# Pair 2's second product in three one-pass parts, passes ordered by form, and a new order of the steps

## The chip, the cores and the metric

The kernel runs on one core of a Trainium2 chip. The core has five engines that run side by side, each through its own list of instructions in order: TensorE (PE; its weight loads are shown apart as PEld), VectorE (DVE), ScalarE (ACT), GpSimd (POOL) and SyncE (SP, which here only starts DMA transfers). The metric is device time in microseconds, the median of several runs; lower is better.

## The reference

A gated linear recurrence is followed by a feed-forward layer. q, k, v, a_re and a_im have 4 batches, 8 heads, 768 positions and 48 channels in fp32. The weights w_in (384 x 2048) and w_out (2048 x 384) come in float64.

```python
mag = sqrt(a_re**2 + a_im**2);  scale = minimum(mag, 0.999) / (mag + 1e-6)
for t in range(S):                       # complex decay of a 48 x 48 state per batch and head
    S_re, S_im = ar*S_re - ai*S_im + k[t] v[t]^T,  ar*S_im + ai*S_re
    y[t] = q[t] @ S_re
x = y as (3072 tokens, 384)
h = x @ w_in
out = (h / (1 + exp(-h))) @ w_out        # (3072, 384)
```

## The kernel before

**Tiling.** The positions are cut into chunks of 128. There are 24 chunks (4 batches x 6), taken as 12 pairs (p = 0 to 11): chunks 2p and 2p + 1 have the same position in two batches. A chunk n first goes through the recurrence in its chunked form: gates for a pair at a time (steps G0 to Ga: magnitude, log decay, angle), running sums of log decay and angle by TensorE (`L`, `phase`), the floor of the sum (`floor`), its exponentials (`exp`), sine and cosine (`turn`, `trig`), the decayed and rotated k and q (`dk`, `dq`, `K`, `Q`), their transposes (`t`, `T` on TensorE for the first four chunks, then `tk`, `tq` on VectorE and `td` by DMA), the weights product and its mask (`w`, `m`), the output (`y`, put into xT by `x` and `xd`) and the state handed on to the same batch's next chunk (`s`, `ss`, `sd`, `S`).

**Feed-forward.** For a pair (256 tokens) the hidden layer is cut into eight blocks jp of 2 x 128 units. `h:p.jp` is the first product (6 fp32 matmuls of 128x256), `g:p.jp` the silu on ScalarE, `r:p.jp` the second product, which adds to accumulators of 128 tokens (m = 0, 1) by 384 columns. When all eight are added, the accumulators are evacuated and stored.

**Weights.** They are fetched as pairs of 32-bit words (`F`, SP's queue), and made fp32 by ScalarE (`R`, low word) and VectorE (`H`, high word; `J`, joined). 28 blocks are converted so in the first 120 us, in the order in which h and r need them.

**Two forms of the second product.** Pairs below PARTS (line 110) use fp32 matmuls (line 820), then `finish` (line 840) copies and stores. Later pairs split both operands. A head a keeps the high bits of g, the tail is b = g - a, and the difference form is gd = a - 4096 b; for the weights there are coarse = head, fine = 4096 x tail and diff = head - 4096 x tail. With u = a coarse + b fine and v = gd diff, the product is (1 + 1/4096) u - v / 4096, exactly the four terms of head and tail. All six operands are in the one-pass type fp32r, so a block takes three one-pass matmuls per weight tile instead of one fp32 matmul (lines 831, 835, 837). The steps for a block are `ga` (head of g, DVE), `gr` (its cast, ACT), `gb` (tail, DVE), `gc` (difference, DVE), `lw` (the weights' diff, loaded from DRAM over SP's queue) and `r`. The three forms of g have one buffer each (PBUF = 1, line 115) except in the last pair, the loaded diff has two. `ov` (line 846, ScalarE) scales one accumulator into SBUF, `oj` (line 850, VectorE) joins the other to it and stores.

**The weights' parts** are made once per block jp by `wh`, `wd`, `ws` (DVE: head, rest, diff), `wq`, `we` (ACT: coarse, fine) and `wk` (diff to DRAM, SP). fine takes over w2's buffers in a ring of nine, so it waits for the fp32 products that still read them. coarse, diff and the g forms lie in `room("right")` (line 879), in memory that the conversion's buffers give back.

**What sets the order.** The steps stand in one long string of 1861 names (lines 957 to 1098). Going through it, the program gives each step's instructions to their engines' lists; an engine never overtakes in its own list, and a DMA queue is served in order too. Waits come from data and from buffers that are still read. SP's queue holds fetches, loads, stores and the transposes of T alike, so an entry that waits holds those behind it.

Of the kernel before, what the change touches and what calls it, by code (L numbers as in the profile page):

```python
# [11 lines left out]
F32 = mybir.dt.float32  # L12
# [58 lines left out]
def kernel(  # L71
# [32 lines left out]
    Q = 32  # L104
# [5 lines left out]
    PARTS = 3  # L110
# [370 lines left out]
    def sums(n):  # L481

        x = X[n]
        first = n < STRAIGHT
        ps = (p_o if first else p_m).tile([C, DM], F32, tag="o" if first else "m", name=f"L{n}")
        running(ps, n, "l", upto if n < 2 else half, half_r)
        x["ek"] = att.tile([C, DM], F32, tag="L", name=f"L{n}")
        x["L"] = ps

    def floor(n):  # L490
        x = X[n]
        nc.vector.tensor_scalar(out=x["ek"], in0=x["L"], scalar1=L_MIN, scalar2=None, op0=ALU.max)
        x["L"] = x["ek"]

    def decays(n):

        x = X[n]
        x["eq"] = att.tile([C, DM], F32, tag="eq", name=f"eq{n}")
        x["decay"] = x["eq"]
        special(x["eq"], x["L"], AF.Exp)  # L500
        special(x["ek"], x["L"], AF.Exp, scale=-1.0)
# [322 lines left out]
    def result_of_parts(p, jp):  # L824
        x = A[p]
        a, b, d, t = (x[name, jp] for name in ("head", "tail", "gd", "diff"))
        last_ = jp == NJ // 2 - 1
        for m in range(2):
            u, v_ = (x["o"][2 * m + i].rearrange("p n c -> p (n c)") for i in range(2))
            for ji in range(2):  # L830
                nc.tensor.matmul(v_, lhsT=d[:, ji, ts(m, C)], rhs=t[:, ji],  # L831
                                 start=(jp == 0 and ji == 0), stop=(last_ and ji == 1))
            for ji in range(2):
                j = jp * 2 + ji
                nc.tensor.matmul(u, lhsT=a[:, ji, ts(m, C)], rhs=W["coarse"][:, j],  # L835
                                 start=(jp == 0 and ji == 0), stop=False)
                nc.tensor.matmul(u, lhsT=b[:, ji, ts(m, C)], rhs=W["fine", jp][:, ji],  # L837
                                 start=False, stop=(last_ and ji == 1))
# [7 lines left out]
    def o_scaled(p, m):  # L846
        ot = A[p]["ot", m] = moe.tile([C, 2, DM // 2], F32, tag="ot", name=f"ot{p}_{m}")
        nc.scalar.mul(ot, A[p]["o"][2 * m + 1], -FINER)

    def o_joined(p, m):  # L850
        ot, u = A[p]["ot", m], A[p]["o"][2 * m]
        halves = (slice(0, 1), slice(1, 2)) if p == NP - 1 else (slice(0, 2),)
        for i, n in enumerate(halves):
            nc.vector.scalar_tensor_tensor(out=ot[:, n], in0=u[:, n], scalar=1 + FINER,  # L854
# [24 lines left out]
    def room(side):  # L879
        if side not in later:  # L880
            (setup if side == "left" else conversion).close()
# [73 lines left out]
    with tc.manual_schedule():  # L955
        for x in """
                warm:30 re:0 re:1g im:0 e0:0 e1:0 e2:0 e3:0 re:2g hold: im:1 e0:1 e1:1 e4:0 e6:0
                e5:0 L:0 e2:1 e3:1 e4:1 e5:1 e6:1 e7:0 e8:0 q:0g k:0g exp:0 dq:0 warm:20 im:2g
                re:3g F: dk:0 e7:1 e8:1 at:0.0 an:0.0 phase:0 at:0.1 an:0.1 R: im:3g G0:1 turn:0
                trig:0 phase:1 turn:1 trig:1 L:1 exp:1 G5:1 G1:1 rk:0.0 warm:34 rq:0.0 t:0.2 t:0.0  # L960
                rq:0.1 t:0.3 T:0.3 T:0.2 G8:1 rk:0.1 q:1g k:1g dk:1 t:0.1 T:0.1 H: v:0g thirds:0
                rk:1.1 G7:1 rk:1.0 dq:1 ends:0 s:0 S:0 T:0.0 rq:1.1 rq:1.0 G2:1 G3:1 w:0.1 m:0.1
                F: H: R: w:0.0 m:0.0 t:1.1 t:1.3 T:1.3 T:1.1 t:1.2 T:1.2 t:1.0 T:1.0 v:1g G6:1
                G9:1 ends:1 last:0 thirds:1 q:2g v:2g k:2g k:3g s:1 y:0 x:0 w:1.1 w:1.0 G4:1 L:2
                L:3 exp:3 F: F: H: S:1 m:1.1 m:1.0 y:1 x:1 Ga:1 phase:2 phase:3 R: J: J: J: h:0.0
                h:0.1 F: sm:1 F: F: turn:2 last:2 exp:2 trig:2 R: H: dk:2 dq:2 rq:2.0 t:2.2 turn:3
                R: trig:3 rk:2.0 t:2.0 T:2.0 T:2.2 rk:2.1 t:2.1 s:2 dk:3 rq:2.1 t:2.3 rk:3.1 t:3.1
                w:2.0 g:0.1 R: T:2.3 rk:3.0 t:3.0 T:2.1 q:3g dq:3 rq:3.1 t:3.3 ends:2 S:2 rq:3.0
                t:3.2 g:0.0 T:3.1 T:3.0 J: H: J: H: T:3.3 m:2.0 w:2.1 m:2.1 r:0.0 H: w:3.1 T:3.2
                R: m:3.1 thirds:2 y:2 x:2 w:3.0 v:3g s:3 thirds:3 m:3.0 y:3 J: J: r:0.1 ends:3 F:  # L970
                F: F: H: R: R: R: x:3 h:1.0 sm:0 S:3 J: H: J: H: J: h:1.2 F: F: R: R: F: g:1.0 H:
                H: J: J: lk:0 lk:1 h:0.3 g:0.3 r:1.0 R: H: J: F: F: g:1.2 h:1.1 g:1.1 R: R: F: R:
                h:0.2 g:0.2 r:1.1 H: H: J: h:1.3 r:0.2 r:0.3 re:4g re:5g im:4g im:5g G0:2 G5:2
                G1:2 G2:2 H: wh:2 J: J: F: F: R: H: H: J: h:1.4 r:1.2 R: J: g:1.3 h:0.4 r:1.3 F:
                R: F: H: H: G7:2 G3:2 G4:2 L:4 R: J: J: F: F: H: R: J: g:1.4 r:1.4 H: G8:2 G6:2
                G9:2 Ga:2 F: F: F: carry:4 R: J: h:1.5 last:1 last:3 carried:4 phase:4 R: R:
                floor:4 H: H: J: exp:4 H: R: g:0.4 L:5 floor:5 k:4g im:6g q:4g h:0.5 r:0.4 exp:5
                turn:4 trig:4 g:1.5 F: R: g:0.5 J: h:1.7 h:0.7 g:0.7 g:1.7 carry:5 carried:5 dk:4
                phase:5 sm:2 F: R: last:4 ends:4 dq:4 J: K:4 tk:4 Q:4 tq:4 H: H: J: ends:5 F: R:
                turn:5 trig:5 k:5g lk:2 r:0.5 h:0.6 r:1.5 h:1.6 g:0.6 r:0.6 J: H: wd:2 we:2 J:  # L980
                dk:5 K:5 q:5g dq:5 Q:5 ws:2 td:4 g:1.6 r:1.6 wq:2 tk:5 tq:5 re:6g re:7g im:7g G0:3
                G8:3 G5:3 G1:3 G2:3 G7:3 G3:3 w:4.0 m:4.0 wh:1 r:0.7 of:0 w:4.1 m:4.1 v:4g s:4 S:4
                G6:3 y:4 x:4 td:5 carry:6 w:5.0 m:5.0 G9:3 w:5.1 m:5.1 v:5g y:5 x:5 q:6g G4:3 L:6
                floor:6 wh:0 wd:0 wh:4 Ga:3 carried:6 exp:6 r:1.7 of:1 wq:0 s:5 S:5 ws:0 xd:2
                h:2.1 wk:2 last:5 q:7g v:8 v:6g k:6g re:8g k:7g g:2.1 wq:1 h:2.0 wq:4 g:2.0
                phase:6 h:2.5 h:2.4 L:7 r:2.0 r:2.1 wd:1 ws:1 wk:1 turn:6 sm:3 ends:6 wk:0 last:6
                trig:6 we:0 g:2.5 dk:6 wh:3 K:6 s:6 g:2.4 wq:3 lk:3 dq:6 floor:7 exp:7 carry:7 k:8
                Q:6 carried:7 tk:6 tq:6 wd:4 ws:4 we:1 phase:7 h:2.2 g:2.2 wd:3 ss:6 ws:3 turn:7
                dk:7 trig:7 K:7 h:2.3 g:2.3 r:2.2 r:2.3 r:2.4 r:2.5 im:8g im:9g re:9g G0:4 G8:4
                G5:4 td:6 w:6.0 ends:7 dq:7 Q:7 tk:7 tq:7 we:4 h:2.7 G1:4 wk:4 we:3 wh:6 G7:4 wd:6  # L990
                ws:6 G2:4 G4:4 we:6 G3:4 wh:5 wd:5 m:6.0 G6:4 G9:4 wq:5 q:8 w:6.1 wq:6 m:6.1 y:6
                x:6 wk:3 sd:6 carry:8 Ga:4 q:9 last:7 v:7g s:7 ss:7 td:7 k:9 sd:7 sm:4 h:2.6 g:2.6
                S:6 ul:8 ws:5 w:7.0 m:7.0 w:7.1 m:7.1 g:2.7 we:5 y:7 x:7 wk:6 L:8 carried:8 ut:8
                floor:8 exp:8 S:7 r:2.6 phase:8 turn:8 trig:8 ul:9 lk:4 dk:8 K:8 tk:8 r:2.7 of:2
                xd:3 im:10 h:3.0 L:9 g:3.0 ends:8 dq:8 floor:9 exp:9 wh:7 wq:7 Q:8 tq:8 ga:3.0
                gb:3.0 h:3.1 h:3.2 gr:3.0 gc:3.0 lw:3.0 r:3.0 wk:5 carry:9 carried:9 ut:9 phase:9
                im:11 re:10 re:11 last:8 wd:7 ends:9 dq:9 g:3.1 ga:3.1 g:3.2 lw:3.1 turn:9 td:8
                h:3.4 h:3.3 ws:7 wk:7 k:11 gr:3.1 gb:3.1 gc:3.1 r:3.1 we:7 ga:3.2 dk:9 trig:9 Q:9
                K:9 G0:5 G5:5 w:8.1 w:8.0 gb:3.2 gc:3.2 tk:9 tq:9 g:3.3 g:3.4 ga:3.4 gr:3.2 G1:5
                G7:5 G2:5 h:3.5 lw:3.2 r:3.2 m:8.0 m:8.1 y:8 ga:3.3 gb:3.3 gc:3.3 G3:5 G6:5 G4:5  # L1000
                v:9 s:9 lw:3.3 gr:3.3 r:3.3 carry:10 last:9 td:9 G8:5 G9:5 Ga:5 k:10 carried:10
                ut:10 g:3.5 gb:3.4 gc:3.4 ss:9 x:8 h:3.7 g:3.7 phase:10 turn:10 h:3.6 g:3.6 ga:3.5
                sm:5 lk:5 w:9.0 m:9.0 w:9.1 trig:10 m:9.1 y:9 x:9 gr:3.4 carry:11 carried:11 ul:10
                s:8 ss:8 L:10 ga:3.6 floor:10 exp:10 lw:3.4 r:3.4 re:12 q:10 re:13 ut:11 phase:11
                gb:3.5 im:12 im:13 G0:6 lw:3.5 last:10 xd:4 h:4.1 gr:3.5 gc:3.5 r:3.5 G5:6 G1:6
                G2:6 gr:3.6 g:4.1 h:4.0 g:4.0 ends:10 dq:10 Q:10 dk:10 K:10 gb:3.6 G8:6 lw:3.6
                gc:3.6 r:3.6 tk:10 turn:11 ga:3.7 gr:3.7 tq:10 trig:11 gb:3.7 ul:11 G7:6 G3:6
                h:4.2 L:11 floor:11 exp:11 q:11 sd:8 g:4.2 h:4.3 g:4.3 G4:6 gc:3.7 lw:3.7 r:3.7
# [265 lines left out]
```

## Time and profile before

| | |
|---|---|
| time, median of 3 runs | 638.94 us (638.41 to 641.1) |
| the profiled execution | 642.44 us, of which the span from first to last instruction is 640.7 |
| granted TensorE clock, mean | 0.995 |
| fp32 second product, L820 | 192 records, 487 ns each (a fp32 matmul leaves two) |
| second product in parts, L831, L835, L837 | 288 recorded each (280 and 8 in other buffers), about 338 ns |
| first product, L716 | 1152 records, 381 ns |
| g forms on VectorE | head 426 ns, tail 684, difference 689 |
| g head's cast on ScalarE | 615 ns |
| weights' parts, per block | DVE 624 + 948 + 949 ns, ACT 825 + 834 ns |
| table loads on ScalarE | 77 of 1283 ns |
| DMA | 104.75 MB, mean 163 GB/s |

Busy times are shares of the span. The lengths of matmuls overlap, so the cost of a block is read from the start of one to the start of what follows. L numbers are lines of the kernel.

### The profile page before, as it was taken

What the parts mean: (1) busy time and instruction counts of PE and PEld (TensorE: products, weight loads), DVE (VectorE), ACT (ScalarE), POOL (GpSimd) and SP (SyncE); (2) the same over time, 40 slices, a digit from 0 to 9 for tenths busy, and PEclk for the clock granted to TensorE, in tenths of its full rate; (3) what the DMA queues carried; (4) which work ended last, traced back from release to release, by engine and by line L of the source; (5) the groups of instructions that cost most, each with busy time, mean ns of one, the idle gap of its engine ahead of it and who ended that gap; (6) DMA issues with size and microseconds to landing.
All of it is one profiled execution on the core that took longest, in us unless ns stands there. A gap on an engine that the chain in (4) does not pass through costs nothing.

```text
span 640.7 us, 11617 instructions
## 1 busy us (share of the span) xinstructions
PE 620.5 (97%) x3892; PEld 542.2 (85%) x3892; DVE 513.7 (80%) x875; ACT 417.1 (65%) x629; POOL 214.7 (34%) x368
## 2 busy tenths in 40 slices
PE   6899999999999999999999989999999998999996
PEld 4788876778777999899999979998988998999996
DVE  5998578858788998998999988988987885855744
ACT  7995398486696878939759848659579354323322
POOL 7341201633553325344224453243434422120000
PEclk8999999999999999999999999999999998999999
DMA  9766976756775896795797786897898573797782
GB/s 163 168 162 151 198 181 177 120 104 175 160 127 145 170 184 146 167 184 123 183 182 171 142 166 141 195 185 134 156 202 150 113 158 85 165 212 224 244 249 77
DMA packets 195111, 104.75 MB, mean 163 GB/s; under 512 B 167520, under 2 KB 173240, under 8 KB 195048
## 3 DMA queue, kind: packets, MB, share of 16 engines
q1 hardware_dynamic: 179944, 82.25, 55.7%
q0 software_dynamic: 11648, 17.20, 16.8%
q10 hardware_dynamic: 3456, 4.52, 2.1%
q8 instruction: 32, 0.52, 0.4%
q14 instruction: 31, 0.25, 0.2%
HBM read 77.21 MB, written 7.93 MB: 133 GB/s over the span
## 4 chain that ended last, share of the span: by engine, by line


## 5 line engine op out<-in xcount | busy, mean ns | idle before, releaser
L716 PE MATMUL h<-xT,w 128*128 128x256 f32 x1152 | 264.7, 381 | 1.0 <-DMA xT<-y 0.4
L716 PEld LDWEIGHTS h<-xT,w 128*128 128x128 f32 x1152 | 216.6, 191 | 32.8 <-ACT g L297 2.3
L562 POOL DMA_DIRECT2D T<-sq x120 | 78.2, 659 | 85.5 <-issue 39.4
L297 ACT ACTIVATE g<-h 128x512 f32<-128x512 f32 x96 | 55.8, 595 | 72.5 <-PE h L716 56.6
L291 ACT ACT_TABLE_LOAD x77 | 98.8, 1283 | 3.0 <-DVE ot L854 1.0
L835 PE MATMUL o<-coarse,head 128*128 128x384 f32 x280 | 94.7, 338 | 0.0
L837 PE MATMUL o<-fine,tail 128*128 128x384 f32 x280 | 94.4, 337 | 0.0
L831 PE MATMUL o<-diff,gd 128*128 128x384 f32 x280 | 82.0, 374 | 2.5 <-DMA diff<-w_diffs 2.2
L798 ACT CAST head<-g_head 128x512 fp32r<-128x512 f32 x70 | 43.0, 615 | 61.3 <-PE o L835 40.6
L508 POOL DMA_DIRECT2D dec<-ends x48 | 30.6, 643 | 138.0 <-DMA ends<-eq 133.0
L802 DVE TENSOR_TENSOR tail<-g,g_head 128x512 fp32r<-128x512 f32 x70 | 47.9, 684 | 29.8 <-PE o L837 29.4
L820 PE MATMUL o<-w,g 128*128 128x384 f32 x192 | 65.0, 487 | 0.0
L831 PEld LDWEIGHTS o<-diff,gd 128*128 128x128 f32 x280 | 50.5, 188 | 7.5 <-DVE kr L529 2.4
L820 PEld LDWEIGHTS o<-w,g 128*128 128x128 f32 x192 | 36.2, 190 | 22.4 <-DVE w L49 0.2
L574 PEld LDWEIGHTS a<-T 96*128 96x128 f32 x384 | 47.1, 191 | 6.7 <-issue 2.9
L837 PEld LDWEIGHTS o<-fine,tail 128*128 128x128 f32 x280 | 52.8, 189 | 0.0
L835 PEld LDWEIGHTS o<-coarse,head 128*128 128x128 f32 x280 | 52.7, 188 | 0.0
L574 PE MATMUL a<-T 96*128 96x128 f32 x384 | 48.9, 276 | 3.7 <-DMA re<-in_a_re_dram 1.8
L690 POOL DMA_DIRECT2D S<-ssq x84 | 47.0, 567 | 13.5 <-DVE ssq L679 11.3
L731 DVE SCALAR_TENSOR_TENSOR gd<-tail,g_head 128x512 fp32r<-128x512 f32 x70 | 48.2, 689 | 1.9
L582 DVE TENSOR_TENSOR w<-a,upto_r 128x512 f32<-128x512 f32 x48 | 32.3, 684 | 11.6 <-PE a L574 11.4
L613 POOL DMA_DIRECT2D xT<-y x30 | 15.0, 506 | 70.2 <-ACT y L649 70.2
(130 smaller groups left out, 985.5 us busy)
## 6 DMA issues: line engine op xcount, KB each, us to landing
diff<-w_diffs SPq DMA_DIRECT2D x72, 384.0 KB
T<-sq SPq DMA_DIRECT2D x120, 64.0 KB
T<-sq POOLq DMA_DIRECT2D x120, 64.0 KB, 4.2
raw<-in_moe_w_out_dram SPq DMA_DIRECT2D x16, 384.0 KB
small<-in_moe_w_in_dram SPq DMA_DIRECT2D x16, 384.0 KB
small<-in_moe_w_out_dram SPq DMA_DIRECT2D x16, 384.0 KB
raw<-in_moe_w_in_dram SPq DMA_DIRECT2D x24, 192.0 KB
out_dram<-ot ACTq DMA_DIRECT2D x22, 192.0 KB
```

Source lines behind the costliest of these rows:

```text
L291: nc.scalar.preload_act_table_set(SETS[of][0])
L297: nc.scalar.activation(out=out, in_=in_, func=func, **kw)
L562: (nc.gpsimd if a % 2 else nc.sync).dma_start(out=to[ts(b, Q), :, a], in_=X[n]["sq"][ts(a, Q), b])
L574: nc.tensor.matmul(ps[:, h], lhsT=x["kT"][:, hh * HH + h], rhs=x["qT"][:, hh * HH + h], start=True, stop=True)
L690: (nc.gpsimd if g % 2 else nc.sync).dma_start(out=to[ts(b, Q), r, :, e], in_=sq[ts(g, Q), :, b, 0:e.stop - e.start])
L716: nc.tensor.matmul(ps[:, ji], lhsT=w1[:, dc, ts(jp * 2 + ji, C)], rhs=A[p]["xT"][:, dc], start=(dc == 0), stop=(dc == ND - 1))
L731: nc.vector.scalar_tensor_tensor(out=dst, in0=tail, scalar=-1 / FINER, in1=whole, op0=ALU.mult, op1=ALU.add)
L802: nc.vector.tensor_tensor(out=t, in0=A[p]["g", jp], in1=A[p]["temp", jp], op=ALU.subtract)
L820: nc.tensor.matmul(A[p]["o"][m].rearrange("p n c -> p (n c)"), lhsT=A[p]["g", jp][:, ji, ts(m, C)], rhs=w2[jp][:, ji], start=(j == 0), sto ...
L831: nc.tensor.matmul(v_, lhsT=d[:, ji, ts(m, C)], rhs=t[:, ji], start=(jp == 0 and ji == 0), stop=(last_ and ji == 1))
L835: nc.tensor.matmul(u, lhsT=a[:, ji, ts(m, C)], rhs=W["coarse"][:, j], start=(jp == 0 and ji == 0), stop=False)
L837: nc.tensor.matmul(u, lhsT=b[:, ji, ts(m, C)], rhs=W["fine", jp][:, ji], start=False, stop=(last_ and ji == 1))
```

## The change

- PARTS is 2 instead of 3: pair 2's second product is done in parts as well (43 steps more in the list: the forms and loads of its eight blocks, `ov` and `oj` in place of `of:2`).
- A block's passes go by form: for both token halves first the heads, then the tails, then the differences. In the last block of the last pair the order is by halves, and by form within a half. Before, each half had its differences first, and then heads and tails in turn.
- `ov` now scales u (heads and tails) by 1 + 1/4096, and `oj` joins v; before it was the other way round.
- The buffer ek is allocated in `floor` (or `exp`), not in `sums`.
- `room` closes the set-up's buffers for either side, and for the right side the conversion's too.
- The list of steps is new throughout, with the weights' parts made about one pair sooner: all but the last two blocks' before `r:2.0`, and those while pair 2 runs. Apart from pair 2's steps both lists hold the same names.

```diff
-    PARTS = 3
+    PARTS = 2
...
         running(ps, n, "l", upto if n < 2 else half, half_r)
+        x["L"] = ps
+
+    def floor(n):
+        x = X[n]
         x["ek"] = att.tile([C, DM], F32, tag="L", name=f"L{n}")
-        x["L"] = ps
-
-    def floor(n):
-        x = X[n]
...
     def decays(n):
...
+        if "ek" not in x:
+            x["ek"] = att.tile([C, DM], F32, tag="L", name=f"L{n}")
...
-        for m in range(2):
-            u, v_ = (x["o"][2 * m + i].rearrange("p n c -> p (n c)") for i in range(2))
+        forms = ((a, lambda ji: W["coarse"][:, jp * 2 + ji]), (b, lambda ji: W["fine", jp][:, ji]),
+                 (d, lambda ji: t[:, ji]))
+        ends_here = last_ and p == NP - 1
+        for n, m in [(n, m) for m in range(2) for n in range(3)] if ends_here else [
+                (n, m) for n in range(3) for m in range(2)]:
+            left, right = forms[n]
+            to = x["o"][2 * m + n // 2].rearrange("p n c -> p (n c)")
             for ji in range(2):
-                nc.tensor.matmul(v_, lhsT=d[:, ji, ts(m, C)], rhs=t[:, ji],
-                                 start=(jp == 0 and ji == 0), stop=(last_ and ji == 1))
-            for ji in range(2):
-                j = jp * 2 + ji
-                nc.tensor.matmul(u, lhsT=a[:, ji, ts(m, C)], rhs=W["coarse"][:, j],
-                                 start=(jp == 0 and ji == 0), stop=False)
-                nc.tensor.matmul(u, lhsT=b[:, ji, ts(m, C)], rhs=W["fine", jp][:, ji],
-                                 start=False, stop=(last_ and ji == 1))
+                nc.tensor.matmul(to, lhsT=left[:, ji, ts(m, C)], rhs=right(ji),
+                                 start=(jp == 0 and ji == 0 and n != 1),
+                                 stop=(last_ and ji == 1 and n != 0))
...
-        nc.scalar.mul(ot, A[p]["o"][2 * m + 1], -FINER)
+        nc.scalar.mul(ot, A[p]["o"][2 * m], 1 + FINER)
...
-            nc.vector.scalar_tensor_tensor(out=ot[:, n], in0=u[:, n], scalar=1 + FINER,
+            nc.vector.scalar_tensor_tensor(out=ot[:, n], in0=v_[:, n], scalar=-FINER,
...
-            (setup if side == "left" else conversion).close()
+            setup.close()
+            if side == "right":
+                conversion.close()
```

Three places of the new list, at the start, where pair 2's second product begins, and at the end:

```diff
+                re:0 e0:0 re:1g im:0 e1:0 e2:0 e4:0 e3:0 e5:0 warm:30 L:0 e0:1 e6:0 e7:0 im:1 e1:1
+                e2:1 e4:1 e8:0 e3:1 exp:0 warm:34 e6:1 e7:1 e5:1 L:1 hold: F: H: e8:1 at:0.0
...
+                h:2.1 g:2.1 we:6 sm:3 lk:3 ga:2.0 gr:2.0 h:2.2 g:2.2 ends:7 v:9 wk:4 lw:2.0 gb:2.0
+                gc:2.0 r:2.0 h:2.3 carry:7 carried:7 dq:7 K:6 phase:7 v:7g tk:6 ends:6 dq:6 lw:2.1
...
+                ck2:0 ck3:0 ck4:0 h:11.4 g:11.4 ga:11.4 gr:11.4 r:11.6 gb:11.4 gc:11.4 lw:11.4
+                r:11.4 ga:11.5 gr:11.5 ga:11.7 gb:11.7 gc:11.7 gb:11.5 gc:11.5 lw:11.5 r:11.5
+                lw:11.7 gr:11.7 r:11.7 ov:11.0 ov:11.1 oj:11.0 oj:11.1
```

## The prediction

> **What bounds the kernel now.** I read the page's busy rows and slices first: which engine has no room, and where?
>
> ```profile
> PE 620.5 (97%) x3892; PEld 542.2 (85%) x3892; DVE 513.7 (80%) x875; ACT 417.1 (65%) x629; POOL 214.7 (34%) x368
> ...
> PE   6899999999999999999999989999999998999996
> ...
> DVE  5998578858788998998999988988987885855744
> ...
> PEclk8999999999999999999999999999999998999999
> ```
>
> TensorE is the bound. Its 20.2 us of idle time lie mostly at the two ends: 7.5 us before 30 us, and the last 4.5. VectorE (DVE) comes second, with 8s and 9s from slice 15 to 31. A busy PE is also the wrong row for a saving, since matmuls overlap: one is recorded with 338 ns but the next starts 175 ns later. So I took starts from TensorE's timeline (start, length, operation), here three stretches of it:
>
> ```profile
> 63.79 7.93 PE L716 MATMUL h<-xT,w 128*128 128x256 f32 x36
> 71.56 2.74 PE L820 MATMUL o<-w,g 128*128 128x384 f32 x8
> ...
> 174.92 10.48 PE L820 MATMUL o<-w,g 128*128 128x384 f32 x32
> ...
> 601.07 2.75 PE L716 MATMUL h<-xT,w 128*128 128x256 f32 x12
> ...
> 605.75 2.75 PE L716 MATMUL h<-xT,w 128*128 128x256 f32 x12
> ```
>
> Three h blocks take 71.56 - 63.79 = 7.77, so 2.59 each. Four fp32 second-product blocks run from 174.92 to the next work at 185.24: 2.58 each, 8 records per block because a fp32 matmul is recorded twice. From 601.07 to 605.75 stand one h block and one block in parts, 4.68 together, so a block in parts takes 2.09.
>
> **PARTS 3 to 2.** Pair 2's eight blocks go from 2.58 to 2.09 us: 8 x 0.49 = **-3.9 us** of TensorE, which is full here, so this counts whole if its operands come in time. A rule speaks against it. The Trainium skill (TensorE: Matmul & The Clock Gate, LDWEIGHTS; Part 3) gives a weight load of 128 columns about 107 ns and lets it overlap a running matmul only where row groups differ; ours use all rows. A block in parts has 12 loads and 12 passes, a fp32 block 8 loads and 8 double passes. Exposed, four more loads would cost 4 x 0.107 = 0.43 and leave 8 x 0.06 = 0.5 us of the gain. The row decides: 12 loads of 188 ns are 2.26 us and would not fit in the 2.09 us that the whole block takes, so they overlap. I keep 3.9.
>
> Its operands cost VectorE 8 x (0.426 g_head + 0.684 tail + 0.689 gd) = 14.4 us, and 1.1 for two joins; ScalarE 8 x 0.615 casts = 4.9, less two table loads of 1.28 (75 in the new order, 77 before); SP eight more loads of 384 KB (3.1 MB on 104.75). Moving the weights' parts adds nothing in sum (VectorE 0.62 + 0.95 + 0.95 for each of eight) but puts some 20 us of it before 140 us, where DVE had room (13.3 of 20 us busy between 120 and 140). A ScalarE wait of 5.6 us goes, where fine waited for a fp32 block; ScalarE is not on the path, so 0. One wait is added: pair 3's first block needs the four o tiles that pair 2 now fills (it filled two). Some 13 us of TensorE work stand between in the new list, against 2 x 0.49 and 2 x 0.55 us of evacuation: 0.
>
> **Passes by form.** The twelve passes stay, so no TensorE time. What changes is when each operand is due: heads at the block's start, tails 0.7 us later, differences and the loaded diff 1.4 us later; before, differences came first. The one stall that this touches is in the timeline (in brackets: idle before, and its end), and it costs more than its length:
>
> ```profile
> 528.03 0.44 PE L604 MATMUL y<-T,S 96*64 96x128 f32 x4
> 530.64 0.59 PE L831 MATMUL o<-diff,gd 128*128 128x384 f32 x2 [2.18 <-DMA diff<-w_diffs]
> ...
> 533.36 3.86 PE L716 MATMUL h<-xT,w 128*128 128x256 f32 x12
> 536.86 0.52 PE L831 MATMUL o<-diff,gd 128*128 128x384 f32 x1
> ```
>
> After it, block and h take 536.86 - 530.64 = 6.22 instead of 4.68: 1.54 us more, at a granted clock of 0.53 in the windows from 532.1. The same page (Part 1) lets the clock fall only after an idle window of about 3.4 us; by it this stall costs 2.2, by the row 2.2 + 1.5 = 3.7. I use the row, though the idle 1.78 us at 381 left the clock at 1.00: the edge lies between. In the new form 1.4 us of the wait are covered by heads and tails, 0.8 stays and would not throttle: **-3.0 us**. The loads move in the new list, so this is a likelihood, between 0 (another operand is late there) and -3.7. Form buffers are single: head and tail come free 1.3 and 0.7 us sooner, gd 0.7 later. Diff's two buffers are also freed later, which holds SP's queue (65.0 us of it already waits on these passes) by up to 0.5 us per block; queued behind are T's transposes, loads and carries. I take 0, since most of these stand several blocks ahead of their reader.
>
> **The end.** The scaling reads heads plus tails, complete two passes (0.35 us) before the end; today it reads the differences, complete four before it. Already now the last join waits for it:
>
> ```profile
> 635.59 0.49 ACT L848 ACTIVATE ot<-o 128x384 f32<-128x384 f32 x1 [0.56 <-PE o L831]
> ...
> 636.34 0.62 DVE L854 SCALAR_TENSOR_TENSOR ot<-o,ot 128x192 f32<-128x192 f32 x2 [0.41 <-ACT ot L848]
> ```
>
> So **+0.35 us**. Block 11.5's tail and gd are now queued behind those of 11.7: from the end of h 11.4, 0.8 us of silu and three heads and five tails or gd in a row (3 x 0.4 + 5 x 0.65) give 5.3 us, where TensorE arrives after two blocks and a heads pass, 2 x 2.1 + 0.7 = 4.9. That is 0.4 us late, like today's wait of 0.37 at 631.4: 0.
>
> **The start.** The DVE work before the first h is the same plus turn 2 (1.1 us) ahead of the first three joins, and DVE is busy 9.9 of 10 us between 30 and 40 now; ScalarE has one decay pair (1.03) and one conversion (0.67) more ahead of the second xT copy. The k wait of 1.2 us goes, since a high part takes its place, which may itself wait for its load. Between -1 and +2: **+1.0**. Moving ek's allocation from sums to floor only lets L start sooner: 0.
>
> **VectorE in pairs 2 and 3.** For every step of both lists I added the mean durations of its rows, by engine (sums for DVE scaled by 0.95, as the whole list gives 542 against the 513.7 measured). From block 1.7 to the first weights product of chunk 10, DVE has 107 us for 124 of TensorE before, and 125 for 128 after: 97%. What the trace shows together with a full TensorE is less:
>
> ```profile
> 300.00:320.00 20.00, 20.00 (x111) 18.69 (x110) 19.09 (x32) 15.83 (x23) 8.97 (x16) 1.00 0.72 167
> 320.00:340.00 20.00, 19.91 (x180) 18.39 (x179) 18.16 (x35) 11.32 (x20) 5.24 (x9) 1.00 1.07 182
> 340.00:360.00 20.00, 20.00 (x103) 18.32 (x102) 18.64 (x30) 19.28 (x26) 13.30 (x23) 1.00 0.74 147
> 360.00:380.00 20.00, 20.00 (x154) 18.17 (x153) 19.12 (x35) 10.78 (x18) 6.24 (x13) 1.00 0.76 167
> ```
>
> The columns after the length are PE, PEld and DVE: 75.0 of 80 us, 94%, with PE at 79.9. At 94% the stretch would take 133, or +5; with DVE able to run ahead on about 18 us of slack at its start, 0. Nearer to zero, as slack comes first: **+1.0**.
>
> **Sum.** -3.9 - 3.0 + 0.35 + 1.0 + 1.0 = -4.55. The profiled execution took 642.44 (span 640.7, 1.7 around it) and would take 637.9. It was 3.5 above the median of 638.94; I take the difference over, so the forecast is **634.4 us**. Less than 0.5% (3.2 us) is about what a measurement cannot tell from no change.
>
> **The rivals.**
> *The stall comes back elsewhere* (chance 0.22). The order is new everywhere, and waits of 1.8 (a DMA), 1.0 and 1.1 us at 382, 437 and 465 show that small ones of any cause occur. Without the 3.0 the sum is -1.6: 637.4. Against it: differences are due last now.
> *VectorE becomes the bound in pairs 2 and 3* (0.14). It decides once its reachable share falls below the demand of 97%. Between 240 and 300 us it was busy 54.4 of 60 (91%), with waits for TensorE in between. At 91%, 125 / 0.91 = 137 us against 128: +9, less 3.9 and with the start and the end (+1.35) 645. For it: single form buffers tie DVE to TensorE's passes (tail waited 29.4 us for them). Against: 94% was reached.
> *All inner stalls go* (0.12). Besides the 3.7 of the stall at 530, the 3.9 us at 382, 437 and 465 vanish and the start costs nothing: -3.9 - 3.7 - 3.9 + 0.35 = -11.2, so 627.8.
> That the parts aren't used for pair 2 is excluded by line 814, which tests the pair against PARTS.
>
> **How the numbers follow.** The forecast's case has 0.52. Its own range is 632 to 637, by the start's and VectorE's bounds, and nine tenths of it lie beyond 0.5%. Faster: 0.47 + 0.12 = 0.59; same: 0.05 and the first rival, 0.27; slower 0.14. The range of 629 to 641.5 takes in the first rival, the forecast's ends, half of the last case and the mild third of VectorE's.
>
> **What would show it.** L820 with 128 records and block spacing still 2.58; pair 2's blocks 2.09 apart. No wait of o's passes for a diff load over 1 us, and no clock digit below 9 after the first slice. The first h near 41 us (40.3 before). The final join 0.35 us further from the last pass. If VectorE binds, waits of TensorE on tail, gd, kr or w appear between 150 and 260 us, with DVE above 19 of 20 in those windows. I am wrong if the blocks in parts are spaced wider where loads and forms run close, or if TensorE's idle time outside both ends grows beyond 7 us.

## The result: 636.4 us, a smaller gain than forecast

The kernel before took 639.03 us in this comparison (16 runs, 636.51 to 643.88), the changed one **636.4 us** (16 runs, 633.84 to 638.88). The ratio is 0.9961, with an interval of 0.9942 to 0.9979. That is some 2.6 us less (0.4%). The direction and the range held; of the 4.55 us forecast, 57% came. Executions over 1.5% above the fastest of their kernel (none of these; below, 7 of 75 of the kernel before on one chip and 1 of e9's 22) are called slow, and ratios and spreads leave them out.

First the page of the changed kernel: its busy row, and three of its rows of slices (40 equal parts of the span, each digit the busy share in tenths, PEclk the granted clock).

```profile
PE 617.1 (97%) x3924; PEld 545.8 (86%) x3924; DVE 524.7 (83%) x901; ACT 419.3 (66%) x635; POOL 216.2 (34%) x368
...
PE   6899999999999999999999999999999999999996
...
DVE  5997899977899999998998979987998876775744
...
PEclk9799999999999999999999999999999999999999
```

The two 8s that TensorE's row had between its ends, and the 8 in the clock's row near 530 us, are gone. The second digit of the clock's row is lower than before, 7 for 9 (16 to 32 us): the forecast's sign of no digit below 9 after the first slice did not come true there. VectorE is busy 11 us longer. TensorE has lost only 3.4 us of busy time. The profiled execution took 635.04 (span 633.2), which is 7.4 below the profiled execution of before, nearly three times what the medians say. That was the first hint that the old profile was not a typical one.

The block in parts, in TensorE's timeline of the changed kernel (start, length, operation):

```profile
158.72 2.75 PE L718 MATMUL h<-xT,w 128*128 128x256 f32 x12
161.12 1.04 PE L838 MATMUL o<-coarse,head 128*128 128x384 f32 x4
162.00 0.87 PE L838 MATMUL o<-fine,tail 128*128 128x384 f32 x4
162.71 0.86 PE L838 MATMUL o<-diff,gd 128*128 128x384 f32 x4
163.40 2.75 PE L718 MATMUL h<-xT,w 128*128 128x256 f32 x12
```

This is pair 2. From h to h it takes 163.40 - 158.72 = 4.68: 2.59 for h and 2.09 for the block, the forecast's number. The order heads, tails, differences can be read off too. The groups of the same kernel (count, busy us and mean ns, idle before with its main releaser) show that the passes found their operands ready:

```profile
L838 PE MATMUL o<-coarse,head 128*128 128x384 f32 x312 | 77.8, 370 | 0.9 <-ACT head L800 0.8
...
L838 PE MATMUL o<-diff,gd 128*128 128x384 f32 x312 | 68.0, 338 | 0.0
L838 PE MATMUL o<-fine,tail 128*128 128x384 f32 x312 | 67.3, 337 | 0.4 <-DVE tail L804 0.4
...
L822 PE MATMUL o<-w,g 128*128 128x384 f32 x128 | 43.2, 487 | 0.0
```

L822 has its 128 records, and the passes of o together waited some 1.3 us. VectorE's demand was met, as the windows of the changed kernel show (window, then its length, PE, PEld, DVE, ACT and POOL busy with the number of instructions, clock, DMA share, GB/s):

```profile
300.00:320.00 20.00, 20.00 (x106) 18.54 (x105) 19.48 (x35) 16.47 (x24) 8.89 (x15) 1.00 0.76 156
320.00:340.00 20.00, 20.00 (x184) 18.76 (x183) 17.30 (x32) 13.10 (x22) 5.98 (x11) 1.00 1.02 202
340.00:360.00 20.00, 20.00 (x102) 18.30 (x101) 19.55 (x32) 16.46 (x23) 12.95 (x24) 1.00 0.64 112
```

Twice VectorE is busy for over 19.4 of 20 us, with TensorE full beside it. Between 160 and 260 us it was busy 92.5 of 100, and TensorE 99.0.

### The profile page after: what moved, and what is told of

It reads as the page before. It is cut to its first block, busy times and chain, and to the rows that moved or that the text cites. A ratio compares the mean times of both kernels' runs of the same rounds, so it can differ in the third digit from the quotient of the medians.

```text
span 633.2 us, 11784 instructions
## 1 busy us (share of the span) xinstructions
PE 617.1 (97%) x3924; PEld 545.8 (86%) x3924; DVE 524.7 (83%) x901; ACT 419.3 (66%) x635; POOL 216.2 (34%) x368
## 4 chain that ended last, share of the span: by engine, by line
PE 45%; DVE 5%; DMA 3%; SPq 2%; ACT 2%; issue 1%; POOL 0%; DVEq 0%; ACTq 0%; POOLq 0%
PE h L718 19%; PE o L838 17%; PE a L576 3%; PE y L603 2%; PE y L606 2%; DMA S<-ssq 1%; SPq L564 1%; DVE sq L557 1%; DMA T<-sq 1%; SPq L173 1%; DVE gd L733 1%; DMA diff<-w_diffs 1%; DVE tail L804 1%; DVE g_head L729 1%; SPq L692 1%
## 5 line engine op out<-in xcount | busy, mean ns | idle before, releaser
L800 ACT CAST head<-g_head 128x512 fp32r<-128x512 f32 x78 | 47.7, 614 | 50.9 <-PE o L838 31.1
L838 PE MATMUL o<-coarse,head 128*128 128x384 f32 x312 | 77.8, 370 | 0.9 <-ACT head L800 0.8
L804 DVE TENSOR_TENSOR tail<-g,g_head 128x512 fp32r<-128x512 f32 x78 | 53.3, 683 | 21.2 <-PE o L838 19.2
L838 PE MATMUL o<-diff,gd 128*128 128x384 f32 x312 | 68.0, 338 | 0.0
L838 PE MATMUL o<-fine,tail 128*128 128x384 f32 x312 | 67.3, 337 | 0.4 <-DVE tail L804 0.4
L733 DVE SCALAR_TENSOR_TENSOR gd<-tail,g_head 128x512 fp32r<-128x512 f32 x78 | 53.8, 690 | 5.0
L838 PEld LDWEIGHTS o<-diff,gd 128*128 128x128 f32 x312 | 55.4, 188 | 0.8 <-DVE gd L733 0.5
L822 PE MATMUL o<-w,g 128*128 128x384 f32 x128 | 43.2, 487 | 0.0
L729 DVE TENSOR_SCALAR g_head<-g 128x512 int32<-128x512 int32 x80 | 33.1, 422 | 6.5 <-ACT g L297 6.5
L822 PEld LDWEIGHTS o<-w,g 128*128 128x128 f32 x128 | 24.2, 190 | 14.9 <-DVE w L49 0.2
```

What stands on the lines that cost most here:

```text
L729: nc.vector.tensor_scalar(out=dst.bitcast(I32), in0=src.bitcast(I32), scalar1=-4096, scalar2=None, op0=ALU.bitwise_and)
L733: nc.vector.scalar_tensor_tensor(out=dst, in0=tail, scalar=-1 / FINER, in1=whole, op0=ALU.mult, op1=ALU.add)
L800: nc.scalar.copy(out=g_form(p, jp, "head"), in_=A[p]["temp", jp])
L804: nc.vector.tensor_tensor(out=t, in0=A[p]["g", jp], in1=A[p]["temp", jp], op=ALU.subtract)
L822: nc.tensor.matmul(A[p]["o"][m].rearrange("p n c -> p (n c)"), lhsT=A[p]["g", jp][:, ji, ts(m, C)], rhs=w2[jp][:, ji], start=(j == 0), sto ...
L838: nc.tensor.matmul(to, lhsT=left[:, ji, ts(m, C)], rhs=right(ji), start=(jp == 0 and ji == 0 and n != 1), stop=(last_ and ji == 1 and n != 0))
```

## The experiments

Each was timed in five rounds beside the kernel before, and the ratios are to the runs of before on the same chip. They are given as recorded and differ a little from the quotient of the two medians (0.9997 against 1.0011 in e1). Three chips were used: one for e1 to e4, one for e5, e6, e7 and e9, one for e10 and e11.

### Was the stall typical? Both kernels again

Nothing is edited here: e1 is the kernel before, e2 the changed one.

> The kernel before once more, for a second profile. The first one (642.44 us) lay 3.4 us above its median of 639.03. Theory A (the 3.7 us that the stall at 530 us and the slower clock after it cost belong to that one execution): a profiled execution near 639 shows no stall of TensorE on a load of diff above 1 us and no slice with a clock below 1.0 after 40 us. Theory B (the stall belongs to the order): it is there again, near 530 us, with some 2 us and the clock near 0.55 after it, and what makes the time vary lies elsewhere. Time: 1.00 of before in either.

> The changed kernel once more, for a second profile. The ratio should come out at 0.996 again (0.994 to 0.998). Start: first first-product block again near 42.0 us, 1.7 later than before, if the new start is slower by its order; near 40.3 if that was chance. Inner idle time of TensorE again below 3 us with no wait on a load of diff.

Measured: e1 637.94 against 637.21 (ratio 0.9997, 0.997 to 1.0024), e2 634.85 (0.9966, 0.9949 to 0.9984). So the gain repeats. e1's profiled execution took 636.76, 0.5 under the median of the 51 runs of before on its chip, so it is not an unusual one. In it (TensorE's timeline, around the place of the old stall):

```profile
528.20 2.75 PE L716 MATMUL h<-xT,w 128*128 128x256 f32 x12
530.61 0.70 PE L831 MATMUL o<-diff,gd 128*128 128x384 f32 x2
...
532.90 2.75 PE L716 MATMUL h<-xT,w 128*128 128x256 f32 x12
```

From h to h it is 4.70 us, no wait for the diff load, and the windows of e1 agree:

```profile
520.00:530.00 10.00, 10.00 (x75) 9.12 (x74) 8.00 (x16) 3.91 (x9) 4.28 (x9) 1.00 0.58 149
530.00:540.00 10.00, 10.00 (x53) 9.35 (x52) 7.81 (x13) 6.17 (x9) 3.90 (x6) 1.00 0.45 115
```

TensorE is full and at full clock, in the same program in which the first profile had a 2.18 us wait and a slow stretch after it. From 40 to 626 us TensorE's idle time was 7.8 in that first profile and 3.7 in e1; in the changed kernel 2.9, and 4.05 in e2. **Two executions of one program differ here by more than the old and the new program do.** The stall belonged to the execution and not to the program: theory A, in the one repeat that there is.

### The parts alone

The new list and pass order, with pair 2 in fp32 again. w2's buffers are gone by then, so it multiplies by fine in w2's place: its output is not the layer's, and only its time counts. The 43 steps of pair 2's forms, loads and joins are left out.

```diff
-    PARTS = 2
+    PARTS = 3
...
-                                 lhsT=A[p]["g", jp][:, ji, ts(m, C)], rhs=w2[jp][:, ji],
+                                 lhsT=A[p]["g", jp][:, ji, ts(m, C)], rhs=W["fine", jp][:, ji].bitcast(F32) if p == 2 else w2[jp][:, ji],
```

> The changed list and passes, but pair 2's second product as one fp32 matmul per weight tile again; its 43 steps for parts are left out, and it multiplies by fine in w2's place, since w2's buffers are given away by then. If the parts of pair 2 are worth their TensorE passes: 8 x 0.49 = 3.9 us more than the changed kernel, its eight blocks 2.58 apart. If VectorE's or SP's relief pays part of it back (15.5 us less on VectorE, eight loads less): 0 to 3 us more. Less than the changed kernel if VectorE was the bound in pairs 2 and 3.

Measured: 639.58, ratio 1.0018 (0.9999 to 1.0037). Its timeline has the block at the fp32 price again, 163.28 - 160.70 = 2.58:

```profile
160.70 2.75 PE L822 MATMUL o<-fine,g 128*128 128x384 f32 x8
163.28 1.03 PE L718 MATMUL h<-xT,w 128*128 128x256 f32 x4
```

Against the changed kernel's 0.9966 and 0.9961 the parts are worth 0.0052 to 0.0057 of 638 us, so **3.3 to 3.6 us** (about 1.6 either way, from the two intervals). The forecast's 3.9 lies within. All else in the change, new list and passes together, shows no gain: +1.1 us (-0.1 to +2.4).

The traces allow a closer reading, from the start of pair 2's first h block to that of pair 3's (a row can merge several blocks). First the changed kernel, then e5:

```profile
153.54 7.93 PE L718 MATMUL h<-xT,w 128*128 128x256 f32 x36
...
203.44 10.52 PE L718 MATMUL h<-xT,w 128*128 128x256 f32 x48
```

```profile
152.93 7.93 PE L718 MATMUL h<-xT,w 128*128 128x256 f32 x36
...
205.55 4.70 PE L718 MATMUL h<-xT,w 128*128 128x256 f32 x21
...
626.71 0.94 PE L838 MATMUL o<-diff,forms 128*128 128x384 f32 x4 [1.68 <-DMA diff<-w_diffs]
```

That is 49.90 and 52.62 us. In e2, e6, e7 and e10, which also have the parts, it is 49.06 to 49.75, so the parts gain 2.7 to 3.6 there, **3.1 on average**. The last line is of the end of e5: a wait of 1.68 us for a diff load. In the changed kernel's two profiles such waits come to 0 and 0.7 us in all. If e5 has it in most executions, the comparison of medians credits the parts with some of it, and the +1.1 for all else is too high by as much; one profile can't tell.

### Passes by form, on either list

e4 gives the old list (and PARTS 3) the new passes and scaling; e3 gives the new list the old ones. The edit is that of the change, made alone and undone alone:

```diff
-        for m in range(2):
-            u, v_ = (x["o"][2 * m + i].rearrange("p n c -> p (n c)") for i in range(2))
...
+        for n, m in [(n, m) for m in range(2) for n in range(3)] if ends_here else [
+                (n, m) for n in range(3) for m in range(2)]:
```

> The kernel before with the passes by form and the new roles of scaling and joining alone; list and PARTS as before. If the passes by form carry the gain of the stall (3.0 us forecast, less 0.35 at the end): 636 to 637, no wait on a load of diff above 1 us near 530. If the stall was one execution's: 639 within 1 us.

> The changed kernel with the old order of passes in a block (per half: differences, then heads and tails in turn) and the old roles of scaling and joining; list and PARTS as changed. If the passes by form are what keeps TensorE from waiting: waits on gd and on loads of diff come back, some 3 to 6 us in sum, 639 to 642 us. If only the list and PARTS matter: 636.4 within 1 us, or 0.35 less by the end.

Measured: e4 642.05 (1.0074, 1.005 to 1.0097), e3 665.67 (1.0431, 1.0388 to 1.0475). Both lie above what was expected. Neither half of the change does without the other. In e3, TensorE's waits and its timeline show why (waits: engine, line, waited for, us in total, times, longest):

```profile
PE o L833 <- DVE gd L733: 21.3, 24, 1.5
```

```profile
309.33 0.62 PE L833 MATMUL o<-diff,gd 128*128 128x384 f32 x2 [1.51 <-DVE gd L733]
```

The new list puts the difference form so late that a block which begins with it stands and waits, 24 times. The wait of 1.51 is about the 1.4 us by which the new order lets differences come later. In e4 the operands are early enough, and the time goes elsewhere. Its waits, TensorE's and those of SP's queue:

```profile
PE a L574 <- DMA S<-ssq: 2.9, 1, 2.9
...
SPq L773 <- PE o L836: 76.9, 33, 6.4
```

SP's queue was held for 76.9 us by loads that wait for a diff buffer (65.0 in the profile of before, 56.6 in e1). TensorE waited 2.9 us for a state at 383 us, where half of the state's transfer goes through SP's queue; the same product had waited 1.8 in before, for another transfer. This profile shows no more than that: it took 639.34 us, 2.7 less than the median of its runs, and its inner idle time is 4.9 us (40 to 626 us), only 1.2 over e1's. Two more orders tell which part of the reordering costs the time.

e9 is the old list with passes by form, but differences first, and with the old scaling:

```diff
-        for m in range(2):
-            u, v_ = (x["o"][2 * m + i].rearrange("p n c -> p (n c)") for i in range(2))
+        for n in range(3):
+            for m in range(2):
...
+                    if n == 0:
+                        nc.tensor.matmul(v_, lhsT=d[:, ji, ts(m, C)], rhs=t[:, ji],
```

> The kernel before with its passes by form as well, but with the differences first (then heads, then tails) and the old roles of scaling and joining; list and PARTS as before. The changed passes cost this list some 5 us, and SP's queue waited 76.9 us for them instead of 56.6 and 65.0. If the diff buffer that comes free late does it, by SP's queue: here it comes free at a third of the block, SP waits under 60 us and the time is 637 or less. If grouping the passes by form is what costs: 640 to 642.

Measured: 638.8, ratio 1.0008 (0.9985 to 1.003), between the two times that were expected. In its waits the hold of SP's queue is shorter than ever:

```profile
SPq L773 <- PE o L834: 48.2, 21, 5.5
```

So grouping by form costs nothing that shows (at most 1.9 us by the interval), and the place of the differences decides on this list: e4 and e9 differ by 0.0066, some 4 us. (They also differ in the scaling and in the chip, but the end of the span is the same in both, 5.5 and 5.7 us after the last pass.) Differences last free diff some 1.4 us later, and the longer hold of SP's queue goes with it; that it is this hold that costs the 4 us is inferred from the two sums, not seen wait by wait.

e11 is the changed kernel with heads, differences, tails:

```diff
-                (n, m) for n in range(3) for m in range(2)]:
+                (n, m) for n in (0, 2, 1) for m in range(2)]:
```

> The changed kernel with the passes by form in the order heads, differences, tails. The diff buffer comes free 0.7 us sooner in each block. If SP's queue, held by the diff loads (81 to 89 us), costs the changed kernel time: SP waits near 60 us for these passes and the time is 1 to 3 us less than the changed kernel's. If the list needs the difference form late: waits of TensorE on gd of 0.3 to 0.7 us in many blocks, 5 to 15 us more.

Measured: 649.28, ratio 1.0167 (1.0119 to 1.0216). In its waits and timeline:

```profile
PE o L838 <- DVE gd L733: 7.4, 11, 1.2
```

```profile
299.80 0.51 PE L838 MATMUL o<-coarse,head 128*128 128x384 f32 x2
301.11 0.98 PE L838 MATMUL o<-diff,gd 128*128 128x384 f32 x4 [0.81 <-DVE gd L733]
```

Even 0.7 us earlier is too early for gd in this list. Differences second give 649 us, last 636; e3's order, which begins each half with them, gave 666: the list is written around an order of passes. SP's queue was held no less here, 85.4 us, and 99.6 in e3, against 81.2 in the changed kernel. On the new list the hold does not follow from the place of the differences alone, so e11 does not tell what it costs.

### The start

The forecast wanted the first h some 1 us later. Old-list kernels have it at 40.29, 40.65, 39.77 and 39.59 (before, e1, e4, e9), new-list ones at 40.93 to 42.09 (seven without e6, mean 41.6): +1.5 us. e6 puts the old list's steps in front, up to about the first h:

```diff
-                re:0 e0:0 re:1g im:0 e1:0 e2:0 e4:0 e3:0 e5:0 warm:30 L:0 e0:1 e6:0 e7:0 im:1 e1:1
...
+                warm:30 re:0 re:1g im:0 e0:0 e1:0 e2:0 e3:0 re:2g hold: im:1 e0:1 e1:1 e4:0 e6:0
```

> The changed kernel with the old list's steps up to the first first-product block, then the changed list's remaining steps in their order. If the new start costs what two profiles of each kernel show (first block at 42.0 and 40.9, before 40.3 and 40.6): first block near 40.4, time 1 us less. If it costs nothing: the same within 0.5 us.

Measured: 635.79, ratio 0.996 (0.9939 to 0.9982), no different from the changed kernel, and its first h stood at 41.39. The aim was missed. Its timeline shows where it fell behind:

```profile
16.62 2.92 PE L439 MATMUL phase<-th,upto_r 128*128 128x384 f32 x4 [3.42 <-DVE th L414]
```

The wait of 3.42 us itself cost nothing: it ends at 16.62, and the 1.93 of before at 16.71. But the granted clock then was 0.50 from 16 to 22 us (1.00 in before), and the four records took 2.92 instead of 1.97. So this run doesn't tell the cost of the new start; that it is near 1.5 us rests on the first h of the other eleven.

### The end

e7 gives the last pair the old scaling, its last block differences first within each half, and puts 11.5's forms ahead of 11.7's. e10 adds an early load of the last diff into an idle xT buffer.

```diff
-        for n, m in [(n, m) for m in range(2) for n in range(3)] if ends_here else [
+        for n, m in [(n, m) for m in range(2) for n in (2, 0, 1)] if ends_here else [
...
-        nc.scalar.mul(ot, A[p]["o"][2 * m], 1 + FINER)
+        end = p == NP - 1
+        nc.scalar.mul(ot, A[p]["o"][2 * m + end], -FINER if end else 1 + FINER)
```

```diff
+        if p == NP - 1 and jp == NJ // 2 - 1:
+            t = moe.tile([C, ND, T], F32R, tag="xT", name=f"diff{p}_{jp}", bufs=2)
```

> The changed kernel with the last pair's last block taking its differences first in each half, scaling and joining in the old roles for that pair, and block 11.5's tail and difference ahead of 11.7's. From the last pass to the span's end 4.4 us instead of 5.6 if the roles cost 1.2 there (0.35 by the scaling, the rest at the store), 5.2 if only the scaling counts. Waits in the last blocks (0.4 to 0.7 us for tail) gone. Time 1 to 1.8 us less in all; the same if the store's landing varies for other reasons.

> The changed kernel with the end of the run before (last block's differences first in each half, old roles for the last pair, 11.5's forms ahead of 11.7's) and the very last diff loaded into the idle xT buffer, asked for ahead of block 11.6's load, so that it doesn't wait for a block's differences. If the last load and the roles are what the end lost: no wait on diff in the last block (1.2 us in the run before), last pass to the span's end 4.3 us, and 1.2 to 1.7 us less than the changed kernel, ratio near 0.994. If the end's gain is lost in the noise: 0.996.

Measured: e7 635.57 (0.9962, 0.9944 to 0.9979), e10 634.83 (0.9953, 0.9932 to 0.9973). From the last pass to the end of the span e7 takes 4.24 us, the changed kernel 5.54. But e7 pays on the way, as its timeline shows:

```profile
626.74 0.58 PE L838 MATMUL o<-diff,gd 128*128 128x384 f32 x2 [1.21 <-DMA diff<-w_diffs]
```

The last differences are now due before their load has landed, and what the end gained is spent there. e10 has no such wait (0.2), yet its end is 5.5 again. e10 has the lowest ratio of all, but the intervals overlap almost wholly, so no better version than the changed kernel is shown.

## Why the forecast was right, and where it failed

**The parts, -3.9: right, at about 3.1.** The spacing is 2.09 as read; they gained 3.3 to 3.6 us by the medians and 3.1 in pair 2's own stretch. The rule that the prediction set against it (the Trainium skill, TensorE: Matmul & The Clock Gate, Part 3: a weight load overlaps running matmuls only where row groups differ) would have left 0.5 us by the prediction's estimate. The same Part also says that a load into the background weight buffer is pulled ahead, which the prediction did not weigh. The trace shows overlap with the same row groups: 12 loads of 188 ns (2.26 us) went into a block of 2.09 us. What lets them overlap, no run here shows.

**The stall, -3.0: the step that failed.** The prediction took 2.18 us of waiting and 1.54 us at a slow clock from one profile and credited their loss to the median ("I take the difference over"). In e1 the same program had neither, so in an ordinary execution there was next to nothing to gain here: TensorE's inner idle time (40 to 626 us) is 3.7 us in e1, and 2.9 and 4.05 in the two profiles of the changed kernel. The profiled execution lay 3.5 us above the median of its three runs, the size of the stall with its slow stretch; that was to be seen in advance.

**The start, +1.0: right in sign,** +1.5 by the first h.

**The end, +0.35: the scaling moved as forecast, the join did not.** The line of the kernel before that decides, its last pass, and the end of the changed kernel:

```profile
635.92 0.33 PE L837 MATMUL o<-fine,tail 128*128 128x384 f32 x1
```

```profile
627.15 0.51 PE L838 MATMUL o<-diff,gd 128*128 128x384 f32 x2
...
627.35 0.49 ACT L850 ACTIVATE ot<-o 128x384 f32<-128x384 f32 x1 [0.55 <-PE o L838]
...
627.87 0.62 DVE L856 SCALAR_TENSOR_TENSOR ot<-o,ot 128x192 f32<-128x192 f32 x2 [0.41 <-ACT ot L850]
```

The last passes end at 636.25 and 627.66. In the kernel before, the last scaling began 0.66 us ahead of that end (at 635.59); now it begins 0.31 ahead, so 0.35 later. But the join began 0.09 us after the last pass before (636.34) and begins 0.21 after it now, only 0.12 later. The prediction read that the join already waited for the scaling. In fact that scaling had ended at 636.08, and the join also needs the last pass, which ended 0.17 later. From the last pass to the span's end it is 5.54 us against 4.45; the other 1 us lies in the landing of the last stores, which the forecast did not have (below).

**VectorE, +1.0: nothing.** In two windows VectorE reached 97.5% beside a full TensorE; the share seen before (94%) was not its limit. From 160 to 260 us the changed kernel's TensorE waited for no tail or gd. That rival (645) fell.

**SP's queue, 0: right for the new list, wrong as a rule.** SP's queue was held 81.2 us in the changed kernel, and the passes of o waited for a diff 0 us there and 0.7 in e2. On the old list the same order cost 4.7 us (e4, 0.0074 of 638).

**The sum.** The parts' 3.3 to 3.6 and the +1.1 that e5 shows for all the rest make -2.2 to -2.5, as measured. In that +1.1 are the start's +1.5 and the end's +1.1, so something returns about 1.5 us; no run isolates it. From the first h to the last pass it takes 590.0 and 590.1 us in e1 and e9, old-list executions without a long stall, and 585.7, 588.2 and 587.2 in the changed kernel, e2 and e6. That is 3.0 less on average, which the parts alone account for: in these executions list and passes gain nothing inside. The spread of the runs offers a candidate for the rest (us):

| chip of | kernel | runs | lowest tenth | median | highest tenth |
|---|---|---|---|---|---|
| e1 to e4 | before | 51 | 635.9 | 637.2 | 640.3 |
| | e4, old list | 22 | 639.5 | 642.0 | 645.3 |
| | changed, e2 | 22 | 633.9 | 634.8 | 637.6 |
| e5 to e9 | before | 68 | 636.2 | 638.4 | 641.5 |
| | e9, old list | 21 | 637.5 | 638.6 | 641.4 |
| | e5, new list | 22 | 637.9 | 639.6 | 640.8 |

The old-list kernels of the table spread over 3.9 to 5.8 us, e2 and e5 over 3.7 and 2.9; e6, also on the new list, has 4.2. Quiet executions of e5 are 1.7 us slower than those of before, and the disturbed ones 0.7 faster. So the new list may lose less to disturbed executions, and that fits stalls like the one at 530, which come in some executions only. That it is these stalls was argued, not shown: only two executions of before were profiled.

**Luck.** That the forecast is off by only 2 us is in part luck. In an ordinary execution the 3.0 us for the stall were not there to gain, and VectorE's 1.0 was not lost; the start and the end cost some 1.2 us more than forecast, and some 1.5 to 2 us came back from a source that no run isolates.

**The rivals.** "The stall comes back elsewhere" has the nearer number (637.4, where 636.4 was measured and 634.4 forecast), but not its mechanism: no wait was over 1 us from the first h on in either profile of the changed kernel, and in e1 there was no stall to come back. That the new list can have one is shown by e5's 1.68 us.

## What to carry to other kernels

Before a stall is counted as a gain, compare the profiled execution with the median: if it is longer by about the stall, profile it once more. An order of passes and a list of steps belong together (each half of this change alone cost 5 to 28 us), so a reorder is to be judged with the list that was made for it. On the old list the pass order also set when buffers came free, and with them how long the queue that refills them was held (48 us or 77).

## What was unexpected of the hardware

- **Idle length alone doesn't decide the clock.** In the profile of before, 2.18 us of idle TensorE at 530 us were followed by a granted clock of 0.57 in the window from 532 to 536. In e4, 2.88 us of idle before 383.39 were followed by 1.00 (windows from 380 to 388). At 10.11 us, behind the same 30 warm-up matmuls, 2.43 us of idle in before were followed by 0.50 (10 to 12) and 3.02 in e6 by 1.00 (the two lines below). So the edge between 1.78 and 2.18 us that the prediction inferred is not there. The window of about 3.4 us that the Trainium skill states (TensorE: Matmul & The Clock Gate, Part 1) agrees with the two longer waits, which kept the clock, and not with the two shorter ones, which lost it.

```profile
10.11 1.65 PE L439 MATMUL L<-l,upto_r 128*128 128x384 f32 x2 [2.43 <-DVE l L373]
```

```profile
10.11 0.91 PE L439 MATMUL L<-l,upto_r 128*128 128x384 f32 x2 [3.02 <-DVE l L373]
```

- **The last store lands in one of two times.** From the last pass to the span's end it is 4.2 to 4.6 us in four runs (before, e1, e3, e7) and 5.4 to 5.8 in the changed kernel, e2, e4, e5, e6, e9, e10 and e11. Between before and the changed kernel most of the difference is in SP's wait at the very end, behind the last stores (1.2 and 2.3 us). The new scaling always had the longer one, the old had both (e9 and e10 long), so what sets it stays open.
- **Executions of one program differ by more than one per cent:** 635.06 to 643.9 us over 27 runs of before on the chip of e10 and e11.
